# A new order of all engines' tasks in the two layers behind an attention, read off by a strict line for each engine

## The chip, the core and the metric

The kernel runs on one core of a Trainium2 chip. The metric is the device time of one execution in microseconds (us). Five engines work side by side: PE (matmuls), DVE (vector), ACT (scalar), POOL (GpSimd) and SP, which here only issues transfers (DMAs). Each engine runs its own list of instructions strictly in the order in which it stands, and waits at its head for semaphores of the others.

## The reference, cut to what is computed

```python
def reference(q, k, v, moe_w_in, moe_w_out, moe2_w_in, moe2_w_out):    # 2 batches, 8 heads, 1152 rows, 64 wide
    q_pool = q.reshape(B, H, S // 2, 2, D).mean(axis=3)                # 576 queries a head
    p = softmax(q_pool @ k.T / 8)                                      # over 1152 keys
    x = heads_side_by_side(p @ v)                                      # 1152 tokens x 512
    h = x @ moe_w_in                                                   # 512 -> 2048
    x = np.maximum(0.01 * h, h) @ moe_w_out                            # 2048 -> 512
    h = x @ moe2_w_in
    return (h * (1 / (1 + np.exp(-h)))) @ moe2_w_out                   # 1152 x 512
```

The weights come as 64-bit floats, the rest as 32-bit floats.

## The kernel before

`attention` (L558) works through eight pairs of heads and leaves x in two tiles, a rounded high part `xh` and the rest `xl`. `mlps` (L1212) then computes the two layers. Every product of two matrices is made of three matmuls, high by high, high by low and low by high, so each operand stands in two tiles.

The two layers are cut into 16 units: layer, a block of 512 of the 2048 hidden columns (four to a layer), and a group of tokens (512 or 640). A unit has an "in" part, hidden values from x, and an "out" part, their product with w_out. The in part of the first block of layer 1 is plain: L1470, 24 matmuls of 128x512 (or 48 of 128x320) for each 128 hidden columns. All other in parts (`cell`, L1498) use a scheme of seven products of half size in place of eight: L1516 on PE into four PSUM places, ACT L1554 copies the first product out, and DVE L1540 adds the others to it, twice into scratch (`late`) and twice into the result (`a`). The seven products need sums of blocks of x: `transform` (L1365) makes them, DVE L1377 (sums of two SBUF tiles), ACT L1392 (their high parts) and DVE or POOL L1398 (the low parts). For layer 1 it reads copies of x that two transfers bring back from memory (`fetch`, L1413: `acc<-kept`, 128 KB, and `late<-kept`, 1 MB).

Hidden values go through `rectify` (L1427): ACT L1443 writes the high part `g` of the activated value, ACT L1448 the whole value into `a` (in the plain part this is the instruction that gives the PSUM place back), and POOL L1438 subtracts the two for the low part. The out part is L1591 in layer 1 and L1657 in layer 2. Its sums over blocks are taken from PSUM by ACT L1608 and L1671 (first block) or DVE L1610 and L1673. ACT L1621 and POOL L1626 split x for layer 2, and SP L1684 sends the output.

While this runs, the weights arrive in 64 loads of 512 KB (L317), and each 128x512 piece is turned from 64-bit to 32-bit floats by bit operations: ACT L341, DVE L345, L349, L353, L360 (0.60 us each), for w_in also ACT L366 and four short DVE sums L380, then ACT L388 and POOL L392 for the high and low part. At the start of the layers the rest of the attention is finished too (`pair_end`, L1693): PE L1014 sums, ACT L1020, DVE L1023 (reciprocal), PE L1027, DVE L1034, ACT L1035, DVE L1036, and for three earlier pairs DVE L1043, ACT L1044, DVE L1045.

What sets the order: each of the two functions fills a `Plan` (L412) with tasks, each with an engine, a cost and a due time. `Plan.run` plays the plan with its own costs and emits the instructions in the order in which they begin there. An engine of the plan that is free takes, of its ready tasks, the one with the smallest due time (`rank`, L466). The due times are two tables of numbers, `DUES`, one number for each task. The emitted order is what runs on the chip. PSUM places (`duo`), scratch (`sc`), tiles `a` and `g` and the buffers of the weights are rings that a task takes and another gives back.

## Time and profile before

| | before |
|---|---|
| median of three runs | 606.61 us (605.55 to 607.59) |
| the profiled execution | 607.19 us, of which its span 605.3 |
| PE busy | 586.3 us (97% of the span) |
| DVE, ACT, POOL busy | 495.3, 331.9, 358.0 us |
| the two layers | about 211.6 to 605.3 us of the span |
| granted TensorE clock | 1.00, that is the 2.4 GHz level, in every slice |

The span runs from the first to the last instruction, and 1.9 us of the execution lie around it. An engine's busy time says little by itself here: what counts is where PE, the busiest one, stands still, and which engine it waits for there.

### The profile page before, as it was taken

What the parts mean: (1) busy time and instruction counts of PE and PEld (TensorE: products, weight loads), DVE (VectorE), ACT (ScalarE), POOL (GpSimd) and SP (SyncE); (2) the same over time, 40 slices, a digit from 0 to 9 for tenths busy, and PEclk for the clock granted to TensorE, in tenths of its full rate; (3) what the DMA queues carried; (4) which work ended last, traced back from release to release, by engine and by line L of the source; (5) the groups of instructions that cost most, each with busy time, mean ns of one, the idle gap of its engine ahead of it and who ended that gap; (6) DMA issues with size and microseconds to landing.
All of it is one profiled execution on the core that took longest, in us unless ns stands there. A gap on an engine that the chain in (4) does not pass through costs nothing.

```text
span 605.3 us, 11529 instructions
## 1 busy us (share of the span) xinstructions
PE 586.3 (97%) x4444; PEld 500.5 (83%) x4444; DVE 495.3 (82%) x797; ACT 331.9 (55%) x573; POOL 358.0 (59%) x257
## 2 busy tenths in 40 slices
PE   8899998999999988999999999998999999999997
PEld 6668666686677667999999999898898988988896
DVE  5798788898989978968988978998987798898343
ACT  3748455576475555756545546656765753644231
POOL 7938676476683155877465555787954564546320
PEclk9999999999999999999999999999999999999999
DMA  7222532454143214233333223312332332332102
GB/s 235 79 79 62 157 81 81 108 185 129 19 133 115 76 42 150 82 106 106 104 97 111 74 70 106 103 36 71 104 106 73 103 104 81 96 104 70 42 28 88
DMA packets 34751, 57.44 MB, mean 95 GB/s; under 512 B 13804, under 2 KB 15240, under 8 KB 34696
## 3 DMA queue, kind: packets, MB, share of 16 engines
q1 hardware_dynamic: 34552, 56.50, 30.7%
q8 instruction: 35, 0.57, 0.4%
q10 hardware_dynamic: 144, 0.20, 0.1%
q14 instruction: 20, 0.16, 0.1%
HBM read 50.99 MB, written 3.60 MB: 90 GB/s over the span
## 4 chain that ended last, share of the span: by engine, by line
PE 77%; DVE 10%; DMA 4%; ACT 3%; issue 3%; POOL 2%; SPq 1%; DVEq 0%; ACTq 0%; POOLq 0%
PE psum L1516 24%; PE psum L1657 16%; PE psum L1591 16%; PE psum L865 10%; PE psum L923 6%; DVE late L909 3%; DVE mx L740 3%; PE psum L734 2%; ACT e L871 2%; DMA wraw<-in_moe_w_in_dram 1%; DMA knat<-in_k_dram 1%; PE psum L1470 1%; DVE wt L360 1%; DMA row<-mn 1%; DMA d<-cmp 1%
## 5 line engine op out<-in xcount | busy, mean ns | idle before, releaser
L1591 PE MATMUL psum<-g,wout 128*128 128x320 f32 (+1 forms) x576 | 102.8, 336 | 2.2 <-ACT a L1448 2.2
L740 DVE TENSOR_REDUCE mx<-psum 128x2 f32<-128x768 f32 x96 | 88.1, 952 | 19.5 <-PE psum L734 11.8
L1657 PE MATMUL psum<-wout,g 128*128 128x512 f32 (+1 forms) x444 | 103.2, 385 | 0.4 <-DVE a L1540 0.2
L1591 PEld LDWEIGHTS psum<-g,wout 128*128 128x128 f32 x576 | 92.0, 188 | 9.5 <-ACT a L1448 2.5
L871 ACT ACTIVATE e<-psum 128x512 f32<-128x512 f32 (+1 forms) x144 | 86.0, 657 | 19.3 <-PE psum L865 17.5
L1657 PEld LDWEIGHTS psum<-wout,g 128*128 128x128 f32 x444 | 80.3, 188 | 16.0 <-DVE late L1540 0.7
L909 POOL TENSOR_TENSOR late<-late,e 128x512 f32<-128x512 f32 (+1 forms) x37 | 53.9, 1457 | 34.6 <-DVE late L909 22.5
L923 PE MATMUL psum<-e,vnat 128*64 128x256 f32 (+1 forms) x576 | 73.2, 408 | 0.0
L1540 DVE TENSOR_TENSOR late<-psum,late 128x256 f32<-128x256 f32 (+3 forms) x84 | 54.8, 653 | 21.9 <-PE psum L1516 19.6
L392 POOL TENSOR_TENSOR wout<-wt,wout 128x512 fp32r<-128x512 f32 x32 | 43.0, 1348 | 42.9 <-ACT wout L388 42.7
L923 PEld LDWEIGHTS psum<-e,vnat 128*64 128x64 f32 x576 | 40.0, 137 | 28.8 <-issue 1.5
L1438 POOL TENSOR_TENSOR g<-a,g 128x512 fp32r<-128x512 f32 (+1 forms) x34 | 50.8, 1503 | 20.7 <-ACT a L1448 18.4
L909 DVE TENSOR_TENSOR late<-late,e 128x640 f32<-128x640 f32 (+1 forms) x73 | 61.4, 881 | 0.6
L392 POOL TENSOR_TENSOR w<-wt,w 128x896 fp32r<-128x896 f32 (+1 forms) x18 | 39.2, 2178 | 34.1 <-ACT w L388 31.0
L1438 POOL TENSOR_TENSOR g<-late,g 128x512 fp32r<-128x512 f32 (+1 forms) x28 | 39.9, 1436 | 26.6 <-ACT late L1448 25.1
L1516 PE MATMUL psum<-xh,w 128*128 128x256 f32 (+1 forms) x224 | 50.5, 296 | 1.6 <-ACT late L1554 1.6
L865 PE MATMUL psum<-qh,kh 64*128 64x320 f32 (+1 forms) x288 | 48.1, 329 | 2.3 <-DVE mx L740 1.2
L1516 PE MATMUL psum<-xh,more 128*128 128x256 f32 (+1 forms) x224 | 49.3, 294 | 0.0
L345 DVE TENSOR_SCALAR psum<-psum 128x512 f32<-128x512 f32 x59 | 40.8, 692 | 7.4 <-ACT psum L341 7.4
L392 POOL TENSOR_TENSOR more<-wt,more 128x896 fp32r<-128x896 f32 x14 | 29.8, 2133 | 26.8 <-ACT more L388 20.7
L341 ACT ACTIVATE psum<-wraw 128x512 f32<-128x512 f32 x59 | 36.9, 626 | 15.8 <-DMA wraw<-in_moe_w_out_dram 10.2
L865 PE MATMUL psum<-row,onesr 64*128 64x320 f32 (+1 forms) x288 | 42.9, 292 | 0.9 <-DMA row<-mn 0.9
(127 smaller groups left out, 1365.8 us busy)
## 6 DMA issues: line engine op xcount, KB each, us to landing
wraw<-in_moe_w_in_dram SPq DMA_DIRECT2D x32, 512.0 KB, 4.1
wraw<-in_moe_w_out_dram SPq DMA_DIRECT2D x32, 512.0 KB, 3.3
vnat<-in_v_dram SPq DMA_DIRECT2D x8, 576.0 KB, 5.6
knat<-in_k_dram SPq DMA_DIRECT2D x7, 576.0 KB, 4.5
qnat<-in_q_dram SPq DMA_DIRECT2D x7, 576.0 KB, 6.0
out_dram<-acc SPq DMA_DIRECT2D x8, 256.0 KB, 3.9
xl<-late SPq DMA_DIRECT2D x7, 288.0 KB, 2.8
xh<-d SPq DMA_DIRECT2D x14, 144.0 KB, 3.6
```

Of the source, the lines that this page charges most:

```text
L345: nc.vector.tensor_scalar(out=tf, in0=tf, scalar1=2.0, scalar2=W_TOP, op0=ALU.max, op1=ALU.min)
L392: self.nc.gpsimd.tensor_tensor(out=lo, in0=tf, in1=hi, op=ALU.subtract)
L740: nc.vector.tensor_reduce(out=mx[p][:, u, c], in_=ps[:, :, 0:KC], op=ALU.max, axis=AX.X)
L865: nc.tensor.matmul(out=ps[:, j, 0:n], lhsT=lhsT[own[j], :], rhs=rhs[own[j], cs], start=m == 0, stop=m == len(terms) - 1)
L871: nc.scalar.activation(out=e_t[h, t], in_=ps[:, :, 0:n], func=ACTF.Exp, scale=scale)
L909: e.tensor_tensor(out=a, in0=e_t[h, 0] if t == 1 else a, in1=e_t[h, t], op=ALU.add)
L923: nc.tensor.matmul(out=vps[h][0][own[j], 0, 0:CW[c]], lhsT=vnat[p][:, j, t, :], rhs=e_t[h, t][:, j, :], start=(t == 0), stop=(t == NKT - 1),)
L1438: (nc.vector if fast else nc.gpsimd).tensor_tensor(out=gl, in0=a(), in1=gh, op=ALU.subtract)
L1516: nc.tensor.matmul(out=box[key][:, bank, 0:n], lhsT=w[:, i, :], rhs=y, start=(kk == 0 and q == 0), stop=(kk == 1 and q == 2),)
L1540: nc.vector.tensor_tensor(out=to, in0=p, in1=y, op=ALU.add)
L1591: nc.tensor.matmul(out=box[x][:, c, 0:n], lhsT=wt[:, ms], rhs=y[:, c * n:(c + 1) * n], start=(f == 0 and y is gh and wt is oh), stop=(f == ...
L1657: nc.tensor.matmul(out=box[x][:, c, 0:n], lhsT=y[:, ts], rhs=wt[:, cs], start=(f == 0 and y is gh and wt is oh), stop=(f == FB - 1 and y i ...
```

## The change

Both tables of `DUES` are replaced by tables of whole numbers, which are places in a line. `Plan.run` sorts each engine's tasks by them, and a free engine may now take only the first task of its line and waits for that one. Three parameters of the plan's cost model are set, and the model of the first loads in attention is altered.

```diff
-    stay_mode=0.0,
-    stay_port=0.0,
+    stay_mode=129.57,
+    stay_port=42.33,
-    stay=0.0,
+    stay=60.0,
@@ DUES
-    name: [int(x) / 100 for x in text.split()] for name, text in dict(attention="""
-0 50 300 0 130 110 280 62 0 193 62 124 186 248 53 402 437 566 601 969 1069 691 1152 626 769 524 591 678 869 981 1242
+    name: [int(x) for x in text.split()] for name, text in dict(attention="""
+0 1 5 0 3 2 4 0 0 1 1 2 3 4 0 1 2 2 4 10 8 7 12 5 8 3 6 6 9 0 0 10 9 7 4 6 1 3 6 7 7 8 2 4 3 5 9 10 11 12 8 10 9 11 13
...
 """, mlps="""
-150 450 210 472 756 883 1013 1092 1193 272 821 948 1082 1265 1344 1536 1082 1676 1910 2034 2176 2318 2398 2476 1334
+1 1 0 0 2 5 7 14 3 2 4 6 12 13 19 5 0 16 17 20 21 22 25 7 2 24 27 28 29 30 33 36 35 13 4 31 34 35 37 38 38 39 41 19 5
...
@@ Plan.run
+        line = {e: [t["n"] for t in self.tasks if t["engine"] == e] for e in self.ENGINES}
+        for e in self.ENGINES:
+            line[e].sort(key=lambda n: (-self.tasks[n]["due"], -n))
...
-                can = [t for t in ready[e] if t["at"] <= now and all(self.can(x, t["take"].count(x)) for x in t["take"])]
+                first = line[e][-1] if self.dues and e != "-" and line[e] else None
+                can = [
+                    t for t in ready[e]
+                    if first in (None, t["n"]) and t["at"] <= now and all(self.can(x, t["take"].count(x)) for x in t["take"])
+                ]
...
+                line[e].remove(t["n"])
@@ attention
-        return dict(lag=lag - 1.1, w=1.7) if p < 3 else dict(lag=lag)
+        return dict(lag=lag + 0.9 * (p == 1), w=2.0) if p < 3 else dict(lag=lag)
```

The instructions are the same in number and kind. In attention every engine's order stays as it is: the first 1806 matmuls, 255 instructions of DVE, 224 of ACT, 116 of POOL and 151 transfers stand as before. In the two layers most of what stands on DVE, ACT and POOL moves by a few places, and PE goes back and forth between in and out parts more often (145 stretches of one line where there were 99). The changed file is shorter, so its line numbers are lower, by 55 in the weight steps (L341 is L286, L388 is L333, L345 is L290) and by 47 in what the layers do (L1443 is L1396, L1377 is L1330, L1554 is L1507). The names are tiles; a number behind one tells buffers apart.

The first place is ACT at the start of the layers, from the end of attention on, before and then changed:

```order
L949 ACTIVATE late<-psum 128x320
L388 ACTIVATE wout_2734<-wt 128x512
L341 ACTIVATE psum<-wraw 128x512 x2
L1044 ACTIVATE xh<-acc_2730 128x576
L1443 ACTIVATE g_2740<-psum 128x512
L1448 ACTIVATE a<-psum 128x512
L1443 ACTIVATE g_2741<-psum 128x512
L1448 ACTIVATE a<-psum 128x512
L1044 ACTIVATE xh<-acc_2730 128x576
```

```order
L902 ACTIVATE late<-psum 128x320
L286 ACTIVATE psum<-wraw 128x512
L333 ACTIVATE wout_2734<-wt 128x512
L286 ACTIVATE psum<-wraw 128x512
L1396 ACTIVATE g_2740<-psum 128x512
L1401 ACTIVATE a<-psum 128x512
L997 ACTIVATE xh<-acc_2730 128x576
L1396 ACTIVATE g_2741<-psum 128x512
L1401 ACTIVATE a<-psum 128x512
L973 ACTIVATE late<-psum,tiny 128x288
```

One weight step (L286) goes ahead of the first high part, and the first activated value (L1401, before L1448) goes ahead of the split of x (L997, before L1044).

SP at the same place, the transfers behind attention, before and then changed:

```order
L605 DMA xh<-d_2719 64x576 x2
L1413 DMA acc_2730<-kept 128x4x64
L317 DMA wraw<-in_moe_w_out_dram 128x1024
L1413 DMA late<-kept 128x4x512
L317 DMA wraw<-in_moe_w_in_dram 128x2x512 x4
```

```order
L558 DMA xh<-d_2719 64x576 x2
L262 DMA wraw<-in_moe_w_out_dram 128x1024
L1366 DMA acc_2730<-kept 128x4x64
L262 DMA wraw<-in_moe_w_in_dram 128x2x512
L1366 DMA late<-kept 128x4x512
L262 DMA wraw<-in_moe_w_in_dram 128x2x512 x3
```

The 1 MB copy (`late<-kept`) now stands behind the first load of a w_in piece.

The second place is DVE where layer 1 ends, at about 392 to 402 us of the trace of before, before and then changed:

```order
L1540 TENSOR_TENSOR late<-psum,late 128x320
L353 SCALAR_TENSOR_TENSOR psum<-wraw,psum 128x512
L1377 TENSOR_TENSOR acc_2730<-acc_2730 128x2x256
L1540 TENSOR_TENSOR late<-psum,late 128x640
L1377 TENSOR_TENSOR acc_2730<-acc_2730 128x2x256
L360 SCALAR_TENSOR_TENSOR psum<-wraw,psum 128x512
L1540 TENSOR_TENSOR a<-psum,late 128x640 x2
L380 TENSOR_TENSOR wt<-psum,wt 128x128
L380 TENSOR_TENSOR wt<-wt,psum 128x128 x2
L380 TENSOR_TENSOR wt<-psum,wt 128x128
L1377 TENSOR_TENSOR acc_2730<-acc_2730 128x2x256
```

```order
L1493 TENSOR_TENSOR late<-psum,late 128x320
L1330 TENSOR_TENSOR acc_2730<-acc_2730 128x2x256 x2
L1493 TENSOR_TENSOR late<-psum,late 128x640
L305 SCALAR_TENSOR_TENSOR psum<-wraw,psum 128x512
L1330 TENSOR_TENSOR acc_2730<-acc_2730 128x2x256 x2
L1493 TENSOR_TENSOR a<-psum,late 128x640
L290 TENSOR_SCALAR psum<-psum 128x512
L1493 TENSOR_TENSOR a<-psum,late 128x640
```

All four sums for layer 2 (L1330, before L1377) now stand ahead of the two sums into `a` (L1493, before L1540), where two of them stood behind.

The third place is ACT where layer 2 begins, at about 411 to 422 us of the trace of before, before and then changed:

```order
L1621 ACTIVATE xh<-acc_2730 128x320
L388 ACTIVATE wout_2739<-wt 128x512
L1392 ACTIVATE th<-acc_2730 128x2x320
L1443 ACT_TABLE_LOAD
L1443 ACTIVATE g_2742<-late 128x512
L1448 ACTIVATE late<-late 128x512
L341 ACTIVATE psum<-wraw 128x512
L1392 ACTIVATE xh<-acc_2730 128x2x320
L1554 ACTIVATE late<-psum 128x256
```

```order
L1574 ACTIVATE xh<-acc_2730 128x320
L1345 ACTIVATE th<-acc_2730 128x2x320
L1345 ACTIVATE xh<-acc_2730 128x2x320
L1507 ACTIVATE late<-psum 128x256
L286 ACTIVATE psum<-wraw 128x512
L1345 ACTIVATE th<-acc_2730 128x2x320
L1396 ACT_TABLE_LOAD
L1396 ACTIVATE g_2742<-late 128x512
```

The copy out of PSUM (L1507, before L1554) now stands ahead of the load of the new activation's table and of the values that follow it.

## Rows read from the trace of the kernel before

**Rows 1.** The page, its head: busy us, share of the span, instructions

```profile
span 605.3 us, 11529 instructions
...
PE 586.3 (97%) x4444; PEld 500.5 (83%) x4444; DVE 495.3 (82%) x797; ACT 331.9 (55%) x573; POOL 358.0 (59%) x257
```

**Rows 2.** PE's waits from 205 to 605: waited for, us, times, longest

```profile
PE psum L1591 <- ACT a L1448: 2.2, 1, 2.2
PE psum L1470 <- ACT a L1448: 2.1, 1, 2.1
PE psum L1516 <- ACT late L1554: 1.6, 1, 1.6
PE psum L1470 <- DVE xl L1045: 0.4, 1, 0.4
...
PE psum L1516 <- DVE late L1540: 0.2, 1, 0.2
```

**Rows 3.** A stretch: us, busy us (count) of PE, PEld, DVE, ACT, POOL, clock

```profile
300.00:350.00 50.00, 50.00 (x331) 47.97 (x330) 44.52 (x82) 27.33 (x45) 27.29 (x18) 1.00 0.31 94
```

**Rows 4.** Timeline of PE, start of the layers: start, us, instruction, idle before

```profile
219.02 0.61 PE L1470 MATMUL psum<-xh,w 128*128 128x512 f32 x2
...
219.70 0.39 PE L1470 MATMUL psum<-xh,w 128*128 128x512 f32 x1
222.16 0.50 PE L1470 MATMUL psum<-xh,w 128*128 128x512 f32 x1 [2.08 <-ACT a L1448]
...
238.78 0.74 PE L1591 MATMUL psum<-g,wout 128*128 128x512 f32 x2 [2.19 <-ACT a L1448]
```

**Rows 5.** Timeline of ACT at the same place

```profile
218.85 0.63 ACT L388 ACTIVATE wout<-wt 128x512 fp32r<-128x512 f32 x1 [6.31 <-DMA d<-cmp]
219.39 1.15 ACT L341 ACTIVATE psum<-wraw 128x512 f32<-128x512 f32 x2
220.48 0.67 ACT L1044 ACTIVATE xh<-acc 128x576 fp32r<-128x576 f32 x1
221.05 0.58 ACT L1443 ACTIVATE g<-psum 128x512 fp32r<-128x512 f32 x1
221.53 0.58 ACT L1448 ACTIVATE a<-psum 128x512 f32<-128x512 f32 x1
```

**Rows 6.** The 1 MB copy's issue, GB/s from 224 to 240, ACT's wait for weights

```profile
225.88 0.37 SPq L1413 DMA_DIRECT2D late<-kept  x1
...
GB/s 0 0 0 0 0 113 184 338 369 348 328 348 358 364 369 358 328 302 404 369 149 56 51 51 41 15 0 0 0 0 0 0 0 0 0 0 0 0 0 0
...
234.66 0.65 ACT L341 ACTIVATE psum<-wraw 128x512 f32<-128x512 f32 x1 [3.04 <-DMA wraw<-in_moe_w_in_dram]
```

**Rows 7.** Timeline of PE where layer 2 begins

```profile
421.02 0.38 PE L1516 MATMUL psum<-xh,w 128*128 128x256 f32 x1 [1.57 <-ACT late L1554]
...
424.33 0.50 PE L1657 MATMUL psum<-wout,g 128*128 128x512 f32 x1 [0.22 <-DVE a L1540]
```

**Rows 8.** Timeline of ACT at the same place

```profile
416.88 1.28 ACT L1443 ACT_TABLE_LOAD   x1
```

**Rows 9.** Timeline of DVE, POOL, ACT and PE where layer 1 ends

```profile
393.46 0.69 DVE L1377 TENSOR_TENSOR acc<-acc 128x512 f32<-128x512 f32 x1
...
395.99 1.55 DVE L1540 TENSOR_TENSOR a<-psum,late 128x640 f32<-128x640 f32 x2
...
398.37 2.18 DVE L1377 TENSOR_TENSOR acc<-acc 128x512 f32<-128x512 f32 x1
...
394.89 1.75 POOL L1398 TENSOR_TENSOR tl<-acc,th 128x512 fp32r<-128x512 f32 x1 [1.62 <-ACT th L1392]
...
397.86 2.15 POOL L392 TENSOR_TENSOR w<-wt,w 128x896 fp32r<-128x896 f32 x1
...
396.57 0.95 ACT L388 ACTIVATE w<-wt 128x896 fp32r<-128x896 f32 x1
...
397.64 1.19 PE L1591 MATMUL psum<-g,wout 128*128 128x320 f32 x7
```

217 rows, old and new, of the table DUES are left out of this document.

## The prediction, made before the changed kernel ran

> **What bounds the kernel now.** I read the head of the page first: PE is busy for 586.3 of 605.3 us, DVE for 495.3 [rows 1]. So PE is what the time is made of, and no new order can shorten its work; it can only take away the places where PE stands still. The view of stretches says where these are not: from 300 to 350 PE is busy all 50.00 us while DVE has 44.52 of work [rows 3]. So inside the layers DVE has work close to PE's without holding it up. The waits of PE from 205 us on, the part that the change reorders, then give nearly all there is: 2.2, 2.1, 1.6, 0.4 and 0.2 us [rows 2], and another 0.2 for a sum of DVE's [rows 7], 6.7 in all. A stop costs a little more than the idle time shown: two matmuls in a row take 0.61 us and one alone 0.39, so one adds 0.22 to a running row, but the end of a row shows 0.17 more than that [rows 4]. I count 0.16 for each stop, so the stops cost 2.24 (2.08 idle), 0.5, 2.35 (2.19 idle), 1.73 (1.57 idle) and 0.38 each for those of 0.22 idle [rows 4, 7]. That is about 8 us, and it is the most that the change can win in the middle of the program.
>
> Three stops lie at the start of the layers (219.9, 226, 236.4), three where layer 2 begins (419.3 to 424.3). They are two separate places, and I follow the new order through each, with the durations of before.
>
> **Start of the layers.** Before, PE runs 36 matmuls of L1470 and needs then a PSUM place that ACT L1448 gives back. ACT does nothing that writes a tile of the layers until 218.85, since these tiles lie where attention's last ones end with a transfer [rows 5]. Nothing in the change moves that point, attention having its old order. Behind it stand L388 and two L341 (0.54 each: 1.09 between the row at 219.39 and the one at 220.48), L1044 (0.57), L1443 (0.48) and then L1448, which begins at 221.53 [rows 5]. In the new order one L341 has gone ahead of the point, where ACT idles 6.31 us, and L1044 behind the first L1448. So L1448 begins 0.54 + 0.57 earlier, at 220.42, and PE goes on at about 221.05 instead of 222.16. But PE's own row has changed too: only 30 matmuls stand ahead of the stop, so PE arrives 6 x 0.23 = 1.36 earlier, at 218.57, and waits 2.48. Three matmuls later L1014 stands, moved up from behind, and needs the place of the second L1448: L1044, L1443 and L1448 behind 220.89 end at about 222.6, and PE waits another 0.87. So the first stop becomes 3.35 in two pieces where it was 2.24. What this buys: the sums of L1014 feed ACT L1020, DVE L1023 and the rest of the normalisation, all of it earlier, so the stop of 0.5 at 226 for L1045 goes. And the third stop goes: there ACT has L341 at its head, waiting 3.04 us for a weight load [rows 6], and the L1448 that PE needs stands behind it. In the new order the two L1448 of that part stand ahead of that L341 and of all L1392; I get about 235.8 for the end of the first, 0.7 before PE needs it. Sum: 2.24 + 0.5 + 2.35 = 5.1 becomes 3.35, a gain of 1.75. It could be 2.4 if L1014's wait is spared by ACT running a little ahead.
>
> The price is on SP and DVE. The 1 MB copy goes behind a 512 KB w_in load, and that load waits for DVE's second L360, which stands later now; I place its issue at 230.0 and the copy's at 230.5. Before, the transfers issued from 225.2 moved their 2.1 MB at about 350 GB/s, most of it in 5.5 us, with a thin tail after it [rows 6]. At this rate 1.5 MB takes 4.3 us from about 231.2, so the copy lands at 235.5 to 236.5, and with such a tail up to 238. DVE's first L1377 now reads this copy and stands ahead of the next conversions. Until 236.3 DVE loses nothing that PE needs. If it lands at 238 and L1377 takes its long form, the chain L1377, L1392 (0.7), L1608 is late by 1.35 and 0.4 at the two PSUM places that L1608 gives back. I take nothing for it in the sum, since the rate is the row's own, and keep 1.75 plus 0.3 for the bad end.
>
> **Where layer 2 begins.** PE stands at 419.3 for ACT L1554, which copies a product that has long been done. ACT is late, since a table load of 1.28 at 416.88 stands ahead of it [rows 8], with L1443, L1448, L341 and L1392 behind the load. In the new order only L1392 twice stands ahead of it and the table load behind. The second L1392 can go when both L1377 are done; L1554 then runs at about 417.6, and PE needs it at 419.3. So the stop of 1.73 goes, and with it the two of 0.38 that come from DVE being late after it: 2.5. The table load now delays an L1443 some us later, for which I allow 0.2 (0 to 0.4).
>
> Ahead of this, at 396, DVE has new work in front of the sums that PE waits for. Before, the two L1540 into `a` run at 395.99, and PE needs their result at 398.23, the fifth of the L1591 that begin at 397.64, 0.147 apart. Now two L1377 stand ahead. What an L1377 costs depends on POOL: 0.69 at 393.46, when POOL does nothing, but 2.18 at 398.37, when POOL began an L392 at 397.86 that ends at 400.01 [rows 9]. The L1377 ends 0.54 after it, as if it had stood until POOL let go. The Trainium skill says why, in "SBUF — State Buffer", section "Who interferes with whom": a DVE instruction with two SBUF inputs and a GpSimd instruction that reads SBUF exclude each other for a whole instruction, and whoever begins first keeps the other out. The trace agrees (2.18 against 0.69); without such a rule both new L1377 would take 0.69, the sum would end at 398.2, and this place would give 2.3 in place of 1.0. At 395.99 POOL is in an L1398 until 396.64 [rows 9]. So the first L1377 ends at about 397.2, and at that moment POOL's next L392 gets ready as well: ACT L388, from 396.57 with 0.95, now stands ahead of a short copy and ends near 397.1. If DVE goes first, the second ends at 397.8, the sum at 398.5, and PE waits 0.3. If POOL goes first, 2.15 for L392, the L1377 ends at 399.9, the sum at 400.6, and PE waits 2.4. Nothing in the rows says which; I take the middle, 1.3. Together 2.5 - 1.3 - 0.2 = 1.0 of gain (-0.3 to 2.2).
>
> **The rest.** In between, PE's row is woven anew, with short groups of the out part among the products. I went through its waits by the order: nearly all have their partner done a microsecond or more ahead, about 20 have 0.4 or less. One such event costs 0.38, as at 424.33 [rows 7]. Of the 112 sums L1540, 27 have more conversion work (0.60 a step) directly ahead than before and 37 less, so I allow half an event, 0.2 (0 to 2.0). At the end two full output transfers instead of one stand ahead of the last; I allow 0.2 (0 to 0.6) for it.
>
> The tables alone act: with attention's order unchanged, and with the strict line deciding for every task, the new cost figures of the plan move no instruction, so they cost nothing.
>
> **Sum.** 607.19 (the profiled execution, 605.3 of it the span [rows 1]) - 1.75 - 1.0 + 0.2 + 0.2 = 604.84. That execution lies 0.58 above the median of 606.61, so the forecast is 604.3, a gain of 2.3 us or 0.4%. About 0.3%, 1.8 us, is what a measurement can tell from no change.
>
> **Rivals.**
> First, a better one: DVE goes first at 397.2, and ACT is ahead at L1014. Then the places give 2.4 and 2.2, and only the end loses: 607.19 - 4.6 + 0.2 - 0.58 = 602.2. For it speaks that both depend on some tenths only. Chance 0.13.
>
> Second, the copy lands late. The gain at the start goes into the wait of DVE for it, 1.75 back: 606.0, the same as before. For it speaks the tail in the GB/s row; against it that the rate ahead of the tail is enough. Chance 0.13.
>
> Third, POOL goes first at 397.2. PE waits 2.4 instead of 1.3, since nothing on DVE passes an L1377 that stands still: 605.4. For it speaks the row at 398.37, where POOL had begun 0.5 ahead; against it that the L1377 which ends at 397.2 needs no signal to be followed by the next. Chance 0.14, the same or barely faster.
>
> Fourth, slower: the woven row. DVE has 44.52 us of work in 50 [rows 3], so a sum behind one more conversion comes 0.60 later, and PE, which now comes back to the products after three matmuls where it stayed away longer, meets it late. If two thirds of the 27 sums with more ahead do so, that is 18 x 0.38 = 6.8, in place of my 0.2: 604.3 + 6.6 = 610.9. It decides from about 6 events on, where the gain of 2.3 is used up. Against it: the average work ahead of a sum is as before, and 37 have less. Chance 0.15.
>
> My forecast has 0.45, and its own spread is about 603 to 605.
>
> **Chances and range.** Faster by over 0.3%: 0.39 of the forecast, the better one 0.13, 0.04 of the third: 0.56. Same: 0.06 of the forecast, the second 0.13, 0.10 of the third: 0.29. Slower: 0.15. The range goes from 601.6, the better one with nothing lost at the end and one short stop fewer, to 608.0, which holds the copy, POOL and four or five late sums together, and leaves out the upper part of the fourth.
>
> **What would show it.** Right: PE's waits behind 205 us show a stop for L1448 near 218.6 to 221.05, one at L1014 up to 222.6, none near 236 and none for L1554; the L1377 near 396 show 1.2 and either 0.7 or 2.7. Wrong: a wait of PE for L1608 near 243 (the copy), a stop of 2.4 near 398 (POOL), or many waits of 0.2 for L1540 from 250 to 590 with PE below 50.00 in those stretches, the slower case. If PE is nearly without waits and the time is still above 605, the loss lies in the end, behind 602 us.

## The result, and the profile of the changed kernel

| | before | changed |
|---|---|---|
| median of four runs | 606.67 us (605.55 to 607.59) | 601.31 us (600.16 to 601.84) |
| the profiled execution | 607.19 us, span 605.3 | 601.84 us, span 600.1 |
| stops of PE in the two layers, start to start | 8.08 us | 2.10 us |

The change makes the kernel faster: the ratio is 0.991 (0.9888 to 0.9932), 5.4 us. The forecast was 2.3 us of gain, so the direction was right and the size too small by more than half; 601.31 lies just below the range.

The head of the page of the changed kernel answers to [rows 1]. PE has the same work, 586.5 us against 586.3, in a span that is 5.2 us shorter:

```profile
span 600.1 us, 11519 instructions
...
PE 586.5 (98%) x4444; PEld 501.2 (84%) x4444; DVE 494.4 (82%) x797; ACT 330.4 (55%) x573; POOL 353.6 (59%) x257
```

PE's waits from 205 us on (waited for, us, times, longest) answer to [rows 2]:

```profile
PE psum L967 <- issue: 0.6, 1, 0.6
PE psum L1423 <- DVE xl L998: 0.5, 1, 0.5
PE psum L1423 <- ACT acc L1561: 0.2, 1, 0.2
```

Three short waits are left of six, and all three lie before 246 us. From 250 us to the end PE does not stand still at all (a stretch: us, busy us and count of PE, PEld, DVE, ACT, POOL, clock, DMA share, GB/s; [rows 3] has such a row of before):

```profile
300.00:350.00 50.00, 50.00 (x333) 47.99 (x332) 45.26 (x81) 26.67 (x46) 28.71 (x18) 1.00 0.32 96
...
400.00:450.00 50.00, 50.00 (x330) 47.03 (x329) 42.16 (x76) 32.23 (x55) 37.30 (x26) 1.00 0.29 85
...
550.00:594.00 44.00, 44.00 (x246) 39.30 (x246) 21.64 (x32) 11.81 (x19) 9.85 (x8) 1.00 0.13 48
```

I measured each stop as the distance from one matmul's start to the next, less the distance that the same pair has in a running row. In before's trace they are 2.24, 0.51 and 2.35 at the start of the layers and 2.98 at layer 2 (1.73, twice 0.38, and two of 0.26 and 0.24 that are too short for the list of waits). In the changed kernel they are 0.29, 0.79, 0.65 and 0.36 at the start and none at layer 2. The layers, from the first L1470 to the last matmul, took 390.40 and take 384.35 us. So of 6.05 us that went out of the layers, 5.98 are stops of PE. Attention, whose order is the same, took 210.32 and 211.09 from the first matmul to the first L1470; over all seventeen traces it lies between 209.0 and 211.7, so this difference says nothing.

The start of the layers, ACT (start, us, instruction, idle before; answers to [rows 5]):

```profile
217.42 0.63 ACT L333 ACTIVATE wout<-wt 128x512 fp32r<-128x512 f32 x1 [3.61 <-DMA d<-cmp]
217.96 0.61 ACT L286 ACTIVATE psum<-wraw 128x512 f32<-128x512 f32 x1
...
218.98 0.59 ACT L1401 ACTIVATE a<-psum 128x512 f32<-128x512 f32 x1
...
220.51 0.61 ACT L1401 ACTIVATE a<-psum 128x512 f32<-128x512 f32 x1
```

The order is the predicted one, and so are the distances: the first L1401 (L1448 of before) begins 1.56 behind the release by `d<-cmp`, where I had 1.57, and the second ends 3.70 behind it, where I had 3.75. What differs is the release itself. The transfers at the same place, of the changed kernel and then of before (SP's queue; the second row of each waits for the first transfer to land):

```profile
215.69 0.33 SPq L558 DMA_DIRECT2D d<-cmp  x1
217.10 1.09 SPq L558 DMA_DIRECT2D xh<-d  x2
```

```profile
214.93 0.33 SPq L605 DMA_DIRECT2D d<-cmp  x1
218.53 0.45 SPq L605 DMA_DIRECT2D xh<-d  x1
```

Here the same small transfer needs 1.41 us until the next may go, there 3.60. ACT is released 1.73 behind the issue here, and 3.92 there [rows 5].

The end of layer 1, DVE and POOL (answers to [rows 9]), each apart:

```profile
393.69 1.41 DVE L1330 TENSOR_TENSOR acc<-acc 128x512 f32<-128x512 f32 x2
```

```profile
392.46 1.30 POOL L1351 TENSOR_TENSOR tl<-acc,th 128x512 fp32r<-128x512 f32 x1 [1.29 <-ACT th L1345]
395.07 2.14 POOL L337 TENSOR_TENSOR w<-wt,w 128x896 fp32r<-128x896 f32 x1 [1.30 <-ACT w L333]
```

The two new L1330 (before L1377) take 1.41 together, two of their short form, because POOL is idle from 393.76 to 395.07. And where layer 2 begins, ACT (answers to [rows 8]) does the copy out of PSUM 2.4 us ahead of the table load:

```profile
414.46 0.39 ACT L1507 ACTIVATE late<-psum 128x256 f32<-128x256 f32 x1
...
416.83 1.28 ACT L1396 ACT_TABLE_LOAD   x1
```

### The profile page after: what moved, and what is told of

It is laid out like the page before. It is cut to its first block, busy times and chain, and to the rows that moved or that the text cites. A ratio compares the mean times of both kernels' runs of the same rounds, so it can differ in the third digit from the quotient of the medians.

```text
span 600.1 us, 11519 instructions
## 1 busy us (share of the span) xinstructions
PE 586.5 (98%) x4444; PEld 501.2 (84%) x4444; DVE 494.4 (82%) x797; ACT 330.4 (55%) x573; POOL 353.6 (59%) x257
## 4 chain that ended last, share of the span: by engine, by line
PE 81%; DVE 10%; DMA 3%; issue 2%; ACT 2%; SPq 1%; POOL 1%; DVEq 0%; ACTq 0%
PE psum L1469 26%; PE psum L1610 16%; PE psum L1544 15%; PE psum L818 11%; PE psum L876 7%; DVE mx L693 4%; DVE late L862 3%; PE psum L687 2%; PE psum L1423 1%; DMA knat<-in_k_dram 1%; DMA late<-kept 1%; ACT e L824 1%; PE psum L916 1%; PE psum L718 1%; DMA row<-mn 1%
## 5 line engine op out<-in xcount | busy, mean ns | idle before, releaser
L1544 PE MATMUL psum<-g,wout 128*128 128x320 f32 (+1 forms) x576 | 105.1, 336 | 0.0
L1493 DVE TENSOR_TENSOR late<-psum,late 128x256 f32<-128x256 f32 (+3 forms) x84 | 54.7, 654 | 21.7 <-PE psum L1469 17.4
L337 POOL TENSOR_TENSOR wout<-wt,wout 128x512 fp32r<-128x512 f32 x32 | 41.4, 1298 | 51.9 <-ACT wout L333 49.1
L862 DVE TENSOR_TENSOR late<-late,e 128x640 f32<-128x640 f32 (+1 forms) x73 | 63.7, 912 | 0.6
L1391 POOL TENSOR_TENSOR g<-a,g 128x512 fp32r<-128x512 f32 (+1 forms) x34 | 48.3, 1434 | 21.2 <-ACT a L1401 7.0
L337 POOL TENSOR_TENSOR w<-wt,w 128x896 fp32r<-128x896 f32 (+1 forms) x18 | 38.6, 2153 | 24.5 <-ACT w L333 19.7
L290 DVE TENSOR_SCALAR psum<-psum 128x512 f32<-128x512 f32 x59 | 40.8, 691 | 7.3 <-ACT psum L286 7.1
L286 ACT ACTIVATE psum<-wraw 128x512 f32<-128x512 f32 x59 | 37.1, 628 | 16.2 <-DMA wraw<-in_moe_w_out_dram 10.2
L337 POOL TENSOR_TENSOR more<-wt,more 128x896 fp32r<-128x896 f32 x14 | 30.2, 2163 | 24.2 <-ACT more L333 15.2
```

Of the source, the lines that this page charges most:

```text
L290: nc.vector.tensor_scalar(out=tf, in0=tf, scalar1=2.0, scalar2=W_TOP, op0=ALU.max, op1=ALU.min)
L337: self.nc.gpsimd.tensor_tensor(out=lo, in0=tf, in1=hi, op=ALU.subtract)
L862: e.tensor_tensor(out=a, in0=e_t[h, 0] if t == 1 else a, in1=e_t[h, t], op=ALU.add)
L1391: (nc.vector if fast else nc.gpsimd).tensor_tensor(out=gl, in0=a(), in1=gh, op=ALU.subtract)
L1493: nc.vector.tensor_tensor(out=to, in0=p, in1=y, op=ALU.add)
L1544: nc.tensor.matmul(out=box[x][:, c, 0:n], lhsT=wt[:, ms], rhs=y[:, c * n:(c + 1) * n], start=(f == 0 and y is gh and wt is oh), stop=(f == ...
```

## The experiments

Three questions stood: why the first stop is so short, how the gain divides between the start of the layers and the rest, and which instruction of the rest brings it.

**The kernel before, once more.** No edit; one more execution with its trace.

> The kernel before once more, for its trace. Theory A (a load of 16 KB of PE's code sits on one DMA engine while the 4.5 KB transfer d<-cmp at the end of attention lands, at the same place in every execution of this program): d<-cmp is issued near 214.9, DVE L1043 and ACT L388 start about 3.8 us behind the issue as before, and the page of the stretch 214.9 to 218.9 counts one packet of the queue for instructions. Theory B (the 3.8 us are chance of that one execution): they start 1.4 to 2.1 us behind the issue. Time 606.6 under both.

Measured: 605.07 us. `d<-cmp` lands in time here, and the first stop is not there. PE's waits from 205 us on:

```profile
PE psum L1516 <- ACT late L1554: 1.6, 1, 1.6
PE psum L1591 <- ACT a L1448: 0.9, 1, 0.9
PE psum L1470 <- DVE xl L1045: 0.4, 1, 0.4
...
```

SP and ACT of the same execution:

```profile
216.26 0.33 SPq L605 DMA_DIRECT2D d<-cmp  x1
217.69 1.42 SPq L605 DMA_DIRECT2D xh<-d  x2
```

```profile
218.00 0.63 ACT L388 ACTIVATE wout<-wt 128x512 fp32r<-128x512 f32 x1 [4.10 <-DMA d<-cmp]
```

So the first two rows of [rows 2] are one execution's. The same program has there once 2.24 and 2.35 of stops, and once 0 and 1.08. A delay that every execution of before has is out.

**Is the late landing tied to a load of code?** In before's trace a packet of the queue that brings instructions lies 1.4 us behind the issue of `d<-cmp`. I moved that load by cutting two warm-up matmuls into eight (28 instructions more on PE; the width summed is the same):

```diff
-        for _ in range(n):
+        for m in range(n):
...
-                nc.tensor.matmul(
-                    out=box["warm"][0][:, j, :], lhsT=onesr[own[j], :], rhs=zero[own[j], :], start=True, stop=True
-                )
+                w = 64 if n == P["warm"] and 2 * m + j >= 2 * n - 2 else 512
+                for c in range(0, 512, w):
+                    nc.tensor.matmul(
+                        out=box["warm"][0][:, j, c:c + w], lhsT=onesr[own[j], :], rhs=zero[own[j], c:c + w], start=True, stop=True
+                    )
```

> The kernel before, with two of the first warm-up matmuls of 512 columns cut into eight of 64 each, at the start where PE waits for loads: 14 more matmuls, 28 more instructions of PE ahead of everything, no other change of order. Theory A: the load of code comes some 28 instructions (about 3 us) earlier, ahead of d<-cmp, the layers' first writes start 1.4 to 2.1 us behind the issue, PE's first stop in the layers falls from 2.2 to 0.2 or less, and the time falls by 1.5 to 2.2 us, to about 604.7. Theory B: no change, 606.6.

Measured: 605.26 us, ratio 0.9999 (0.9981 to 1.0016). The load moved to 1.2 us ahead of the issue and the landing was in time in the one trace, but the time is that of before; the interval leaves room for 1.2 us of gain, less than the 1.5 to 2.2 that were expected if the load made the stop.

**The changed kernel again, and with its code moved** (one warm-up matmul cut in the same way, 14 instructions more).

> The changed kernel once more. Theory A: d<-cmp lands 1.4 us behind its issue again, PE stops 0.3 and 0.8 us at the start of the layers, 601.3 us. Theory B: the landing differs from trace to trace by up to 2 us. Attention ends 0.77 us later in the trace of the changed kernel than in that of before although its order is the same; if that is chance, here it ends somewhere between 211.3 and 212.4.

> The changed kernel with one warm-up matmul of 512 columns cut into eight of 64, 14 more instructions of PE ahead of everything. In the changed kernel the load of code stands just behind the place where PE stops for L1014, so it comes at 222.2, behind d<-cmp. Theory A: 14 instructions are enough for it to come ahead of that stop, near 216 to 219; if it meets d<-cmp, the layers' first writes start 3 us or more behind the issue and the time rises by 1 to 2.2 us, to 602.3 to 603.5; if it falls behind the landing, nothing changes. Theory B: 601.3.

Measured: 601.18 us, 0.9927 (0.99 to 0.9955), and 600.85 us, 0.992 (0.9891 to 0.9948). In both the landing is in time and the stops sum to 1.71 and 2.08. The load lies more than 6 us behind the issue in all nine traces with the new start, and none of these has a late landing. With the old start it lies 1.0 to 1.4 behind in seven of eight traces, and three of the seven are late. This fits a landing that is held up by the load at times. It isn't shown: moving the load away did not change the median of before, and three in seven against none in nine can be chance.

**The planner's new code and attention's table, with the old order of the layers.** In the changed file the table of the layers holds the places in which the instructions of before stand; the order of the instructions is that of before on every engine:

```diff
 """, mlps="""
-1 1 0 0 2 5 7 14 3 2 4 6 12 13 19 5 0 16 17 20 21 22 25 7 2 24 27 28 29 30 33 36 35 13 4 31 34 35 37 38 38 39 41 19 5
...
+0 0 1 1 4 6 8 11 4 2 5 7 9 11 15 6 1 17 19 21 23 25 25 8 3 20 20 26 28 30 31 34 36 21 4 33 33 35 38 40 42 43 47 19 5
...
```

> The changed kernel with the table of the layers replaced by the places that each task has in the order of before: the new planner code and the new attention table, the old order everywhere. Theory T2 (all of the gain lies in the layers): same as before, 605.1, 7 stops of PE in the layers, 4.6 to 4.9 us in sum, or 8.1 if d<-cmp lands late as in the first trace. Theory T3 (the planner code or attention gives about 1 us): 604.1 or less.

Measured: 605.32 us, 0.9989 (0.9966 to 1.0012). No gain of the rules alone can be told from none, as predicted; the interval ends at 2.1 us below before. The trace showed something else. PE stands for ACT's copy until 418.36, as it does in before, but here the granted clock falls behind that stop (stretches; the clock is the third number from the end):

```profile
418.00:419.00 1.00, 0.64 (x5) 0.64 (x6) 1.00 (x3) 0.91 (x4) 0.22 (x1) 1.00 0.00 0
419.00:420.00 1.00, 1.00 (x7) 0.85 (x7) 1.00 (x3) 1.00 (x2) 0.37 (x1) 0.84 0.02 8
420.00:421.00 1.00, 1.00 (x5) 0.86 (x5) 1.00 (x3) 0.71 (x2) 1.00 (x2) 0.50 0.00 0
421.00:422.00 1.00, 1.00 (x7) 1.00 (x6) 1.00 (x3) 0.34 (x1) 1.00 (x1) 0.50 0.00 0
422.00:423.00 1.00, 1.00 (x4) 0.81 (x4) 1.00 (x3) 0.91 (x3) 1.00 (x2) 0.50 0.00 0
423.00:424.00 1.00, 1.00 (x5) 0.80 (x5) 1.00 (x2) 1.00 (x4) 1.00 (x2) 0.95 0.53 80
```

For 3.4 us PE runs at the 1.2 GHz level. The layers less their stops take 383.6 us in this trace and 382.3 in before's, so this costs some 1.3 us. In the trace that the prediction rests on the clock stays at 1.00 through the same stretch, and nothing there showed that the stop can have this second price.

**Half of the change each.** The new order up to about 300 us of the trace and the old one behind it, and the other way round, by tables of the same kind.

> The new order in the layers up to about 300 us of the trace, the old order of before for all tasks behind that. T1 (as predicted: the start gives 1.75): 1.75 us below before, 603.3. T2 (the stop of 2.2 at the start belongs to a late landing in one execution of before; in others the start has stops of 1.6 to 1.9 before and 1.7 to 2.1 in the changed kernel): the same as before, 605.1, with the stops near 417 to 424 in place (1.73, 0.38, 0.38, 0.26).

> The old order of before in the layers up to about 300 us, the new order behind that. T1 (as predicted: the rest gives 0.6 to 1.0): 604.3. T2: no stop near 396 and none from 417 to 431 or at 545, so nearly the whole gain of the changed kernel, 2.9 us, 602.2; the start keeps its stops of about 0.5 and 1.1 to 1.4.

Measured: the new start alone 604.64 us, 0.9971 (0.9949 to 0.9993); the new rest alone 603.15 us, 0.9957 (0.9935 to 0.998). So the start is worth 1.8 us (0.4 to 3.1) and the rest 2.6 (1.2 to 3.9); each time lies between the two that were expected for it. Together 4.4, where the whole gave 5.4 in its first comparison (4.1 to 6.8) and 4.4 when it was run again (2.7 to 6.1). PE's waits with the new start alone and with the new rest alone:

```profile
PE psum L1469 <- ACT late L1507: 1.6, 1, 1.6
PE psum L967 <- issue: 0.6, 1, 0.6
PE psum L1423 <- DVE xl L998: 0.5, 1, 0.5
```

```profile
PE psum L1423 <- ACT a L1401: 1.6, 1, 1.6
PE psum L1544 <- ACT a L1401: 1.2, 1, 1.2
PE psum L1544 <- POOL g L1391: 0.4, 1, 0.4
...
```

The stop for ACT's copy is in the first and not in the second. The first two rows of the second are the start's old stops (`d<-cmp` took 3.15 here, late again), and the wait for POOL lies at 304, where the two orders meet; neither kernel has it.

**Does one instruction carry the rest?** First the old order with only the copy moved ahead of the table load on ACT:

```diff
 L1345 ACTIVATE th<-acc_2730 128x2x320
+L1507 ACTIVATE late<-psum 128x256
 L1396 ACT_TABLE_LOAD
 L1396 ACTIVATE g_2742<-late 128x512
...
 L1345 ACTIVATE xh<-acc_2730 128x2x320
-L1507 ACTIVATE late<-psum 128x256
```

> The old order of before with one instruction of ACT moved: where layer 2 begins, L1554 (now L1507, the copy out of PSUM that PE waits 1.73 us for) stands ahead of the table load and the four instructions that stood in front of it. If that copy alone holds PE: the stop of 1.73 goes and the two of 0.38 with it, 2.0 to 2.7 below before, 602.4 to 603.1. If DVE is as late as ACT there (its L345 and second pair of L1377 stand ahead of the sums), PE meets the sums instead and the stops come back as several of 0.4 to 1: 604 to 605.

Measured: 606.43 us, 1.0014 (0.9992 to 1.0037), no gain. The copy runs at 414.39, but PE stands longer there than before, now for DVE, which itself waits at the head of its list. PE's waits from 300 us on, and DVE:

```profile
PE psum L1469 <- DVE late L1493: 2.3, 2, 2.1
```

```profile
417.99 0.70 DVE L290 TENSOR_SCALAR psum<-psum 128x512 f32<-128x512 f32 x1 [2.38 <-ACT psum L286]
418.60 0.88 DVE L1330 TENSOR_TENSOR acc<-acc 128x640 f32<-128x640 f32 x1
419.40 0.41 DVE L1493 TENSOR_TENSOR late<-psum,late 128x256 f32<-128x256 f32 x1
```

DVE's next weight step L290 needs ACT's L286, which is still behind the table load, and behind L290 stand the L1330 and the L1493 that PE needs. One wait took the place of the other.

Then the reverse, the changed kernel with only this copy put back behind the load:

```diff
 L1345 ACTIVATE xh<-acc_2730 128x2x320
-L1507 ACTIVATE late<-psum 128x256
 L286 ACTIVATE psum<-wraw 128x512
...
 L1396 ACTIVATE g_2742<-late 128x512
 L1396 ACTIVATE g_2743<-late 128x512
+L1507 ACTIVATE late<-psum 128x256
```

> The changed kernel with one instruction of ACT moved back: where layer 2 begins, L1507 (L1554 before) stands behind the table load and two L1396 again. Theory: a stop of PE of 1.5 to 2.0 us near 416 comes back, and one or two of 0.2 to 0.4 behind it; in some executions the granted clock falls behind the stop, as in runs of before with a mean of 0.997, which costs another 1.3 us. 603.0 to 604.4. Rival: the new order of DVE alone does it, and ACT's place is of no account: 601.2.

Measured: 605.64 us, 0.9991 (0.9971 to 1.0011): with this one instruction moved, no gain over before is left. The time lies above the expected 603.0 to 604.4, since the stop that comes back is 3.2 us and not the 1.6 of before. So the figure is the price of this place in the new order, and not the copy's share of the 5.4. PE's wait, and the stretches around and behind it:

```profile
PE psum L1469 <- ACT late L1507: 3.2, 1, 3.2
```

```profile
416.00:419.00 3.00, 0.00 (x0) 0.00 (x0) 0.14 (x1) 2.97 (x6) 2.44 (x2) 0.96 0.01 3
419.00:422.00 3.00, 2.91 (x13) 2.91 (x14) 2.93 (x5) 1.18 (x3) 2.37 (x2) 0.50 0.25 46
...
423.00:426.00 3.00, 3.00 (x22) 2.88 (x21) 2.65 (x5) 2.52 (x5) 2.31 (x2) 1.00 0.12 45
```

At the 1.2 GHz level PE does 13 matmuls in 3 us, and 22 a little later at the other.

Third, the old order with the start of layer 2 on ACT and DVE (nine instructions each) in the new relative order; ACT's part:

```diff
+L286 ACTIVATE psum<-wraw 128x512
+L1345 ACTIVATE th<-acc_2730 128x2x320
+L1345 ACTIVATE xh<-acc_2730 128x2x320
+L1507 ACTIVATE late<-psum 128x256
 L1345 ACTIVATE th<-acc_2730 128x2x320
 L1396 ACT_TABLE_LOAD
 L1396 ACTIVATE g_2742<-late 128x512
-L1401 ACTIVATE late<-late 128x512
-L286 ACTIVATE psum<-wraw 128x512
-L1345 ACTIVATE xh<-acc_2730 128x2x320
-L1507 ACTIVATE late<-psum 128x256
 L1396 ACTIVATE g_2743<-late 128x512
...
```

> The old order of before everywhere but for one place: where layer 2 begins, nine instructions of ACT (from L1345 to the second L1401; L1392 to L1448 before) and nine of DVE stand among themselves as in the new order, that is, with the copy out of PSUM (L1507) and ACT's L286 ahead of the table load, and DVE's two L1330 ahead of its sums. If these two stretches make the gain of the rest: no stop near 416 to 421, the stops near 429 and 545 (0.26, 0.24) stay, no fall of the clock there: 2.5 plus 0.7 to 1 us below before, 602.5 to 603.3. If the gain needs the woven order of the whole rest: 605 to 606 again, with other stops in the place of these.

Measured: 610.28 us, 1.0053 (1.0034 to 1.0072), slower. The stop for the copy is gone and others stand in its place, most of them for POOL:

```profile
PE psum L1610 <- POOL g L1391: 1.6, 2, 1.3
PE psum L1469 <- POOL tl L1351: 1.4, 1, 1.4
PE psum L1469 <- DVE late L1493: 1.2, 1, 1.2
...
```

The clock is at 0.50 from 423.3 to 430.2 too. POOL's row at the place shows what POOL itself waited for, ACT's L1401, which stands later now:

```profile
419.83 2.52 POOL L1391 TENSOR_TENSOR g<-late,g 128x512 fp32r<-128x512 f32 x2 [4.71 <-ACT late L1401]
```

So the copy's new place is needed, as the run before this shows, but it is not enough, even with its neighbours on ACT and DVE: here the first values of layer 2 come later, and POOL and PE, still in the old order, wait for them. That the new order of PE and POOL makes up the difference is the reading that is left; no run has only that order.

**The landing, made late.** In both kernels the last `d<-cmp` is sent twice, the second behind the first:

```diff
-        x = dma(due, down2, after=[x], lag=P["lag"] - 1.0)
+        def twice():
+            o, i = down2()
+            if p == NP - 2:
+                nc.sync.dma_start(out=o, in_=i)
+            return o, i
+
+        x = dma(due, twice, after=[x], lag=P["lag"] - 1.0)
```

> The kernel before with the last d<-cmp (4.5 KB, the end of attention) sent twice, the second waiting for the first, so that the first writes of the layers are released some 2 us later in every execution. If the late landing made the stops of the first trace of before: PE stops about 2.2 near 219.7 and about 2.4 near 236, stops in the layers 7.5 to 8.5, time about 3.3 us above before, 609.2. If the new end of the landing only moves idle time of ACT: 606.

> The same second transfer in the changed kernel. By the prediction's own sum PE stops 2.5 for the first L1448 (now L1401) instead of 0.3, the stop of 0.8 at L1014 (now L967) stays, the later ones are unchanged: stops of 3.9 to 4.4 in the layers, time 2 to 2.3 us above the changed kernel, 603.4. Then the new start gives 1 us more than the old one when the landing is late, and in sum 4.2 to 5.5 over before with the same second transfer.

Measured: before 607.21 us, 1.0024 (1.0004 to 1.0044), and changed 602.39, 0.9949 (0.9924 to 0.9975). Both lie below the expected 609.2 and 603.4; between them are 4.8 us, within the expected 4.2 to 5.5. In before's trace the first of the two was itself late (216.08 to 219.59, 3.51), the second took 1.40, and the stops at the start are 3.46 and 0.73. Right behind the first of these the clock falls, here at the start of the layers and not at layer 2 (stretches):

```profile
224.00:228.00 4.00, 3.46 (x8) 2.78 (x9) 4.00 (x7) 3.49 (x8) 3.43 (x3) 0.57 0.08 17
228.00:230.00 2.00, 2.00 (x15) 1.06 (x15) 1.59 (x3) 0.94 (x3) 2.00 (x2) 1.00 0.73 227
```

The layers less their stops take 383.7 us, 1.4 more than in before's first trace, about as much as the fall cost behind the stop of layer 2. In the changed kernel the two transfers take 1.42 and 1.41, and the first stop is 1.64 instead of 0.29. In the kernel before, the second transfer cost 1.5 us (0.2 to 2.7 by the ratio). For the changed kernel, which wasn't timed beside it, the ratio is 0.9949 where it was 0.991 and 0.9927, 1.3 to 2.4 us more, with more than 1 us of room to either side. So it is not shown that either order is more robust against a late landing. What does set the two kernels apart is that the traces show a late landing of the first transfer with the old start alone, in three of eight.

**What is left at the start.** The 1 MB copy ahead of the w_in load, and then also the sums L967 three matmuls later on PE:

```diff
 L1366 DMA acc_2730<-kept 128x4x64
-L262 DMA wraw<-in_moe_w_in_dram 128x2x512
 L1366 DMA late<-kept 128x4x512
-L262 DMA wraw<-in_moe_w_in_dram 128x2x512 x3
+L262 DMA wraw<-in_moe_w_in_dram 128x2x512 x4
```

```diff
 L1423 MATMUL psum<-xl,w_60 128x512
+L1423 MATMUL psum<-xh,w_60 128x512 x2
+L1423 MATMUL psum<-xl,w_60 128x512
 L1423 MATMUL psum<-xh,w_60 128x512
 L967 MATMUL psum<-late,ones 32x288 x4
 L1423 MATMUL psum<-xh,w_60 128x512
-L1423 MATMUL psum<-xl,w_60 128x512
-L1423 MATMUL psum<-xh,w_60 128x512 x2
 L1423 MATMUL psum<-xl,w_60 128x512
```

> The changed kernel with the 1 MB copy (late<-kept) ahead of the w_in load on SP again, as in before. The prediction priced the swap at 0 to 1.75 us. DVE's idle time of 1.3 us for the copy before its first L1330 (L1377 before) should go, and with it PE's stop of 0.36 for L1561 (L1608 before) near 245; the load comes later in its place, which ACT's L286 at 236.8 has room for: 600.8 to 601.2. If the load is what DVE needs sooner, 601.5 or more.

> The changed kernel with the 1 MB copy ahead of the w_in load (as in the run before) and the four matmuls of L967 three matmuls later on PE: the stop of 0.8 at L967 falls to 0.1, the normalisation begins at most 0.1 us later, and the stop of 0.62 for DVE's L998 stays. 600.1 to 600.5, 0.7 to 1.1 below the changed kernel. If the 0.8 only moves on to the stop for L998: 600.9.

Measured: 600.85 us, 0.9916 (0.9885 to 0.9946), and 600.58 us, 0.9893 (0.9868 to 0.9917). The first trace has no stop of 0.36 (those of e3 and e10, with the copy still behind, have none either), the second none of 0.79 in addition; 0.28 and 0.72 are left. The second is the fastest of all, by some tenths over the changed kernel, which wasn't timed beside it; the intervals of the two overlap, so only the traces tell them apart, and only for the 0.79.

**POOL's lock at 396.** The changed kernel with POOL's second L1351 back where it stood before, right behind the first:

```diff
 L1351 TENSOR_TENSOR tl<-acc_2730,th 128x2x256
+L1351 TENSOR_TENSOR xl<-acc_2730,xh 128x2x256
 L337 TENSOR_TENSOR w_60<-wt,w_60 128x896
 L1391 TENSOR_TENSOR g_2740<-a,g_2740 128x640
 L1391 TENSOR_TENSOR g_2741<-a,g_2741 128x640
-L1351 TENSOR_TENSOR xl<-acc_2730,xh 128x2x256
```

> The changed kernel with one instruction of POOL moved back to its old place, the second L1351 (L1398 before) of the group near 393, which the new order had put four places later. It then runs at 393.8, just when DVE's third and fourth L1330 (L1377 before) begin. If a DVE subtraction of two SBUF tiles stands still while POOL reads SBUF: one of the two takes about 2.0 us instead of 0.7, the sum into a ends 1.3 later, and PE, which had 0.26 us to spare, stops about 1.0: 602.2. If DVE keeps going first: POOL's L1351 takes 2.0 or more instead and PE does not stop, 601.2.

Measured: 601.99 us, 0.9912 (0.9884 to 0.9939), and DVE and POOL at the place:

```profile
393.88 2.39 DVE L1330 TENSOR_TENSOR acc<-acc 128x512 f32<-128x512 f32 x2
```

```profile
393.92 1.82 POOL L1351 TENSOR_TENSOR xl<-acc,xh 128x512 fp32r<-128x512 f32 x1
```

The two L1330 take 2.39 where they took 1.41, the L1351 1.82 where one alone takes 1.30, and PE waits 0.6 for the sum into `a` (0.73 start to start). The time is near the expected 602.2, but the changed kernel wasn't timed beside it. The mechanism of the prediction exists, at about half of the 1.3 that I had taken for it; the change had moved POOL's instruction out of its way.

## Why the prediction was right or wrong

**The bound: right in kind.** PE's work is the same, and 5.98 of 6.05 us that left the layers are its stops. But I read the stops from one execution as if they were the kernel's: 8.08 us there, and 4.58, 4.87 and 5.58 in the three other traces of before's order (e1, e2, e5).

**The start, 1.75: the size fits, the reasons only in part.** The new first stop was to be 2.48 and is 0.29. Every distance behind the release came out within 0.05; the release was the row [rows 5] of an execution in which `d<-cmp` landed 2.2 us late. So both sides of the subtraction were too high, and that their difference fits is in part luck: the old stops sum to 5.1 there, and to 1.6 to 3.1 in the traces with the usual landing (e1 1.60, e2 1.89, e5 3.11, e8 2.05, e13 2.24); the new ones sum to 1.7 to 2.2, not 3.35. Over seven traces with the old start, two late ones among them, the mean is 2.8 against 2.0, a gain of 0.8; the new start alone was timed at 1.8 (0.4 to 3.1), which holds both this and my 1.75. The wait of L1014 was 0.79 (0.87 predicted), and the third stop went. The stop of 0.5 at 226 did not go, it is 0.65, for POOL's sake. DVE and POOL of the changed kernel there:

```profile
228.78 1.87 DVE L998 TENSOR_TENSOR xl<-acc,xh 128x576 fp32r<-128x576 f32 x1
```

```profile
228.74 1.29 POOL L1391 TENSOR_TENSOR g<-a,g 128x512 fp32r<-128x512 f32 x1
```

POOL began 0.04 ahead, and the L998 ends 0.6 behind POOL's end. Two L998 in a row take 1.43 elsewhere, so this one alone, at 0.7, would be done at 229.5, before PE needs it near 230.0. I had followed this place by ACT and DVE and not by POOL. The 1 MB copy was issued at 229.40 (230.5 predicted), and DVE waited 1.32 for it until 236.17, just under the 236.3 from which I held that PE would notice. PE did stop, 0.36 at 245, but the copy alone does not make that stop. In the five traces that have it, the fourth L1330 behind the copy takes 1.92 to 1.95 beside a POOL instruction; in e3 and e10 DVE waits 1.28 and 1.22 for the copy, that L1330 takes 0.82, and there is no stop.

**Layer 2, 1.0: this is the step that failed.** The new order behind 300 us alone gives 2.6 (1.2 to 3.9), where my terms for it sum to 1.0 - 0.2 - 0.2 = 0.6. Of the terms, 2.5 for the stops was right (2.49 in the trace, and 0.50 in two more that the list did not show). The 0.2 for the table load was 0. The 1.3 for two L1377 ahead of the sums into `a` was 0, and this is the term that failed: the place came out like the case that I had named for no lock at all, 2.3. I had left POOL's L1398 at 394.89 to 396.64 [rows 9], but of its 1.75 us a part is the lock's: an L1377 of DVE runs from 394.79. Once that L1377 stands earlier, L1398 begins at 392.46 and takes 1.30, and the pair in question meets an idle POOL. The race with POOL's next L392 (now L337), which I had priced in the middle, was still near: L337 begins at 395.07, and the pair ends at 395.10. But in all eight traces with the new order at this place the pair takes 1.41. The Trainium skill, "SBUF — State Buffer", section "Who interferes with whom", says that a DVE instruction with two SBUF inputs contends with a GpSimd instruction that reads SBUF; the run with POOL's old place agrees and shows the price (2.39 against 1.41). What failed was the rule's use: a duration that one such instruction had lengthened was kept for an order in which that instruction is elsewhere.

And a term was missing: the fall of the clock at a long stop, some 1.3 us in a trace that has it. How much of the gain it makes is open. A run without a trace has only a mean granted clock, which tells that the clock fell and not where. 40 of the 94 runs of before beside the experiments have a mean of 0.997 or less, and none of the 30 of the changed kernel (with e3) and of e4, e12, e14 and e15, whose traces have no stop above 0.8. But e10, which has a stop of 1.64 at the start and none at layer 2, has such a mean in 4 of 12 runs, and e7, likewise, in 1 of 12; and e9's trace has its fall at the start. So the late landing, too, can bring the fall. In the four groups of runs of before, those with such a mean average 605.35, 607.06, 607.72 and 607.11, the others 604.91, 605.17, 605.31 and 606.52.

**The rest and the end.** 0.2 for late sums was 0: PE is busy all of every stretch from 250 us on, so rival 4, the slower one, had no event. The end lost 0.03 (from 3.28 to 3.31 us behind the last matmul; 0.2 predicted). The planner's code shows no gain of its own (e5).

**The rivals.** Nearest was the first, 602.2, of which half was so: POOL did not come in between at 396, while at L1014 ACT was not ahead. The copy was nearly late, as the second says, for 0.36 instead of 1.75. The third needs POOL's old order, which is not in the changed kernel.

What stays open is why the transfer behind `d<-cmp` can go 1.4 us after it in most traces and only 3.2 to 3.6 after it in three with the old start, and how many of the runs without a trace have this; why one stop of 1.7 us is followed by a lower clock and another of the same length is not; and whether the 1.0 us by which the first comparison exceeds the sum of the two halves is more than noise.

## What to carry to other kernels

Before an order is costed from one trace, take a second execution of the same kernel: a wait that ends with a small transfer can be 2 us of chance, and both sides of the subtraction change with it. Where DVE and POOL lock each other out, a duration from the trace is true only for the neighbour that stood beside it; cost the new order with the undisturbed duration and add the lock where the new neighbours meet. A stop of PE amid dense work should be counted with what the clock may do behind it. And an order is moved as one piece: the instruction that ends a wait was needed here, but alone it gained nothing.

## What the runs showed of the hardware

- A stop of PE of 1.7 us amid busy stretches is followed in some executions by 3.4 us at the 1.2 GHz level (e5), in others by none (the first trace of before, e1). In e11 the fall begins at the end of a stop of 3.2, in e9 at the end of one of 3.3 at the start of the layers, in e13 after several. The length of the stop alone does not decide: the first trace of before has two more stops of 2.24 and 2.35, and e5 one of 2.6 at 236, without a fall.
- The same 64-partition transfer between two tiles was followed by the next one, which waits for it, after 1.40 to 1.43 us in most traces and after 3.15, 3.51 and 3.60 in three.
- Attention, in the same order in all kernels, took between 209.0 and 211.7 us in single traces. This is half of the whole gain, so a part of the program is better judged by its own stops than by the span.
